# Attention and two feed-forward layers on one core: unsplit gate products in extra places, the second batch's gates ahead of out1, new planner numbers

## The chip, the core and the metric

The kernel runs on one core of a Trainium2 chip. The metric is the device time of one launch in microseconds (us), from several runs; beside it stands one profiled execution, whose trace gives start and duration of every instruction on the five engines: TensorE (PE in the rows, PEld for its weight loads), VectorE (DVE), ScalarE (ACT), GpSimd (POOL) and SyncE (SP, which issues DMA transfers).

## What is computed

```python
a = softmax(phi over the sequence)                    # 4 batches, 8 heads, 576 x 32
k_m, v_m = a^T k, a^T v                               # 32 memory rows of 64 a head
attn = softmax(q k_m^T / 8);  x = attn v_m            # to 2304 tokens x 512
xn = x / rms(x) * rms_g
g, val = xn @ w_gate, xn @ w_val                      # 512 -> 1536
x = (silu(g) * val) @ w_out                           # "out1", 1536 -> 512
h = x @ w_in                                          # 512 -> 2048
out = where(h >= 1, h, where(h <= -1, 0, (h + 1)**2 / 4)) @ w_out2
```

The large weights arrive as 64-bit floats and are converted on the chip.

## The kernel before

Every matmul of full precision is made of three: each operand x is kept as a high part (a copy in the rounded format fp32r) and a low part (x minus that copy), and high*high, high*low and low*high are summed. Splitting an operand is thus a copy on ScalarE and a subtraction on VectorE or GpSimd.

**Stages.** Attention runs first, in nine pairs of column blocks; its end product for batch b is the tiles `Ah{b}`, `Al{b}` (high and low of the attention weights, scaled by the rms; `ATp` are the transposes that lead to them, `xp` the products whose squares give the rms). The values `v_m` are folded into the gate and value weights instead of multiplied with attention: `vw` (L738) makes the folded weights `vwps` of two gate blocks and `vw_parts` splits them into `vwh`, `vwl`. `gv` (L783) then forms, for each of 48 gate blocks n (12 a batch, each of 128 hidden columns) and each half hf of the 576 tokens, six matmuls into `gps` and six into `vps` (L806); `gate` (L814) follows each half: Silu on ScalarE into a tile `th` (L831), times `vps` on VectorE (L834), copy to `ah` on ScalarE (L837), subtraction to `al` (L839). `out1` (L847) sums over the 12 gate blocks of a batch, for four column blocks d4 and two halves, in `ops` (L864: three matmuls a block); `x2_parts` splits the result (L878, L880) and stores it to DRAM. The last phase (L1034, L1065) reads that back for the second feed-forward layer.

**Weights.** `convert` (L236) turns 512 columns of 64-bit floats into 32-bit ones. One transfer fills a `raw` tile (four buffers), then: the high word scaled (L258, VectorE or ScalarE), the low word scaled (L261 or L263, ScalarE or GpSimd), an OR of the two (L267, VectorE), and the sign, either by a second VectorE operation (L272) or by a Sign on ScalarE and a product on GpSimd (L277, L279). Where the weight is needed split, copy (L286) and subtraction (L288, VectorE or GpSimd) follow. The 24 gate and value pieces go to tiles `w` and are also stored to `wf_d`; `load_w` (L728) reloads them for later batches. `wo1` (12 conversions through `cx`) is out1's weight; 32 more conversions through `cx` and the tiles `w2s` are the weights of the last phase, stored to `w2_d` and loaded (L967) on GpSimd's DMA queue.

**Who sets the order.** All of this up to the last phase is written as generators that yield (engine, time) or take and give buffers, banks and flags; `Agenda` plays them against a table of engine times and emits each instruction when its turn comes: earliest start first, then the smaller priority (`P_CONV`, `P_VW`, `P_GV`, `P_OUT1`, `P_W2`). Where a step may run on two engines the earlier end wins, shifted by `BIAS`. So numbers in tables decide the order on every engine, and engines run in that order. A gate takes one of 12 `a` buffers (`ah` and `al` of 576 columns) before its matmuls and a `th` buffer of 288 columns; out1's last column block gives the `a` buffers back one by one. Since 12 gates make a batch, no gate of the next batch starts before out1 has begun its last column block.

## Time and profile before

| what | value |
|---|---|
| median of three runs | 873.9 us (872.69 to 874.95) |
| profiled execution: time, span of its trace | 873.91 us, 872.1 us |
| TensorE busy | 831.8 us, 95% of the span |
| VectorE, ScalarE, GpSimd busy | 472.3 us (54%), 351.1 us (40%), 180.3 us (21%) |
| TensorE clock, mean | 0.975 of full |

The shares are means over stages with different limits: attention and the first batch's gates up to some 185 us, out1 with the later gates up to 470, the second layer from there. Matmuls are pipelined, so a busy TensorE is a TensorE that is never without one, not one at its peak.

### The profile page before, as it was taken

What the parts mean: (1) busy time and instruction counts of PE and PEld (TensorE: products, weight loads), DVE (VectorE), ACT (ScalarE), POOL (GpSimd) and SP (SyncE); (2) the same over time, 40 slices, a digit from 0 to 9 for tenths busy, and PEclk for the clock granted to TensorE, in tenths of its full rate; (3) what the DMA queues carried; (4) which work ended last, traced back from release to release, by engine and by line L of the source; (5) the groups of instructions that cost most, each with busy time, mean ns of one, the idle gap of its engine ahead of it and who ended that gap; (6) DMA issues with size and microseconds to landing.
All of it is one profiled execution on the core that took longest, in us unless ns stands there. A gap on an engine that the chain in (4) does not pass through costs nothing.

```text
span 872.1 us, 15148 instructions
## 1 busy us (share of the span) xinstructions
PE 831.8 (95%) x6058; PEld 725.9 (83%) x6058; DVE 472.3 (54%) x817; ACT 351.1 (40%) x695; POOL 180.3 (21%) x207
## 2 busy tenths in 40 slices
PE   7996797689999999999999999999999999999997
PEld 5885586489999999999999888888888888888896
DVE  3679889984776488448512333433343334333443
ACT  1456686762564367447402222222222222222232
POOL 3257656531231222113302300000000000000000
PEclk9998698799999999999999999999999999999999
DMA  9966666855759668766983960100040002000100
GB/s 318 333 209 188 214 203 229 282 190 200 244 207 318 238 241 271 268 224 242 314 274 121 400 210 1 44 5 1 1 130 16 1 1 72 25 1 1 39 11 24
DMA packets 72199, 137.56 MB, mean 158 GB/s; under 512 B 8897, under 2 KB 37569, under 8 KB 72129
## 3 DMA queue, kind: packets, MB, share of 16 engines
q1 hardware_dynamic: 61472, 108.02, 36.8%
q0 software_dynamic: 10496, 28.32, 10.4%
q8 instruction: 47, 0.77, 0.3%
q10 hardware_dynamic: 160, 0.26, 0.1%
q14 instruction: 24, 0.19, 0.1%
HBM read 99.35 MB, written 37.22 MB: 157 GB/s over the span
## 4 chain that ended last, share of the span: by engine, by line
PE 86%; DVE 6%; ACT 3%; DMA 2%; issue 2%; POOL 1%; SPq 0%; DVEq 0%; ACTq 0%; POOLq 0%
PE acc L1065 23%; PE hp L1034 23%; PE ops L864 17%; PE vps L806 7%; PE gps L806 7%; PE vwps L757 2%; PE xp L678 2%; PE sc L615 1%; DMA kv<-in_v_dram 1%; DMA raw<-in_moe_w_val_dram 1%; PE kvps L489 1%; PE qps L597 1%; DVE w L258 1%; DVE w L267 1%; DVE cx L258 1%
## 5 line engine op out<-in xcount | busy, mean ns | idle before, releaser
L1034 PE MATMUL hp<-xh,w 128*128 128x512 f32 (+1 forms) x640 | 193.1, 368 | 0.0
L1065 PE MATMUL acc<-w,gh 128*128 128x512 f32 x576 | 178.4, 391 | 0.0
L1034 PEld LDWEIGHTS hp<-xh,w 128*128 128x128 f32 x640 | 117.0, 188 | 21.5
L1040 DVE SCALAR_TENSOR_TENSOR y<-y 128x512 f32<-128x512 f32 (+1 forms) x80 | 51.1, 639 | 151.6 <-ACT y L1039 151.6
L1065 PEld LDWEIGHTS acc<-w,gh 128*128 128x128 f32 x576 | 107.0, 188 | 22.4
L1034 PE MATMUL hp<-xl,w 128*128 128x512 f32 (+1 forms) x320 | 118.3, 370 | 0.0
L864 PE MATMUL ops<-ah,wo1h 128*128 128x288 f32 x384 | 113.5, 296 | 0.0
L864 PE MATMUL ops<-ah,wo1l 128*128 128x288 f32 x384 | 113.1, 295 | 0.0
L864 PE MATMUL ops<-al,wo1h 128*128 128x288 f32 x384 | 113.0, 294 | 0.0
L1065 PE MATMUL acc<-w,gl 128*128 128x512 f32 x288 | 112.6, 392 | 0.0
L1039 ACT ACTIVATE y<-hp,consts 128x512 f32<-128x512 f32 (+1 forms) x80 | 51.6, 645 | 151.3 <-PE hp L1034 151.3
L1049 ACT ACTIVATE gh<-y 128x512 fp32r<-128x512 f32 (+1 forms) x80 | 47.4, 593 | 137.7 <-PE acc L1065 120.2
L1050 DVE TENSOR_TENSOR gl<-y,gh 128x512 fp32r<-128x512 f32 (+1 forms) x80 | 51.1, 639 | 80.4 <-ACT gh L1049 80.4
L279 POOL TENSOR_TENSOR cx<-cx,raw 128x512 f32<-128x512 f32 x43 | 58.8, 1368 | 128.3 <-ACT raw L277 92.6
L864 PEld LDWEIGHTS ops<-ah,wo1h 128*128 128x128 f32 x384 | 72.0, 188 | 1.6 <-issue 1.6
L864 PEld LDWEIGHTS ops<-al,wo1h 128*128 128x128 f32 x384 | 72.1, 188 | 0.0
L864 PEld LDWEIGHTS ops<-ah,wo1l 128*128 128x128 f32 x384 | 72.0, 188 | 0.0
L1034 PEld LDWEIGHTS hp<-xl,w 128*128 128x128 f32 x320 | 60.2, 188 | 10.8
L806 PE MATMUL vps<-Ah,vwh 128*128 128x288 f32 x192 | 60.1, 313 | 6.7 <-DVE th L834 6.5
L1065 PEld LDWEIGHTS acc<-w,gl 128*128 128x128 f32 x288 | 54.0, 188 | 12.4
L806 PE MATMUL gps<-Ah,vwh 128*128 128x288 f32 x192 | 59.0, 307 | 5.0 <-ACT vwh L775 3.0
L806 PE MATMUL gps<-Ah,vwl 128*128 128x288 f32 x192 | 58.3, 303 | 3.5 <-DVE vwl L777 3.5
(115 smaller groups left out, 1415.1 us busy)
## 6 DMA issues: line engine op xcount, KB each, us to landing
w<-wf_d SPq DMA_DIRECT2D x36, 512.0 KB, 4.8
w<-w_d POOLq DMA_DIRECT2D x36, 512.0 KB, 9.1
w_d<-w2s SPq DMA_DIRECT2D x32, 512.0 KB, 3.5
raw<-in_moe_w_out_dram SPq DMA_DIRECT2D x28, 512.0 KB, 5.5
raw<-in_moe_w_in_dram SPq DMA_DIRECT2D x16, 512.0 KB, 5.3
raw<-in_moe_w_gate_dram SPq DMA_DIRECT2D x12, 512.0 KB, 4.4
raw<-in_moe_w_val_dram SPq DMA_DIRECT2D x12, 512.0 KB, 4.9
wf_d<-w SPq DMA_DIRECT2D x12, 512.0 KB, 3.0
```

What stands on the lines that cost most here:

```text
L258: nc.vector.tensor_scalar(out=dst, in0=hv, scalar1=SHRINK, scalar2=None, op0=ALU.mult)
L279: nc.gpsimd.tensor_tensor(out=dst, in0=dst, in1=hv, op=ALU.mult)
L678: nc.tensor.matmul(out=xp[rows, 256 * g : 256 * g + 256], lhsT=aT[:, i, g, rows], rhs=vbd_t[bb][:, g].rearrange("p h d -> p (h d)"), start ...
L757: nc.tensor.matmul(out=vps[g][0][32 * c : 32 * c + 32, 2 * P * x : 2 * P * x + 2 * P], lhsT=vT[b][hs, c, :], rhs=t[hs, c].rearrange("p i f ...
L806: nc.tensor.matmul(out=p[:, 0:HB], lhsT=wt[:, g, i, :], rhs=at[b][:, g, c], start=(g == 0 and x == 0), stop=(g == 1 and x == 2),)
L864: nc.tensor.matmul(out=p[:, 0:HB], lhsT=wt[:, fc, d], rhs=at[:, c], start=(fc == 0 and x == 0), stop=(fc == NF1 - 1 and x == 2),)
L1034: nc.tensor.matmul(out=hp, lhsT=wt[:, kc, :], rhs=xt[:, kc, 0:n], start=(kc == 0 and x == 0), stop=(kc == KC - 1 and x == 2),)
L1039: nc.scalar.activation(out=y, in_=hp, func=AF.Relu, scale=0.5, bias=half)
L1040: nc.vector.scalar_tensor_tensor(out=y, in0=y, scalar=1.0, in1=y, op0=ALU.min, op1=ALU.mult)
L1049: nc.scalar.activation(out=gh, in_=y, func=AF.Copy)
L1050: nc.vector.tensor_tensor(out=gl, in0=y, in1=gh.bitcast(F32), op=ALU.subtract)
L1065: nc.tensor.matmul(out=acc, lhsT=gt[:, cs], rhs=wt, start=(fc == 0 and x == 0), stop=(fc == NF2 - 1 and x == 2),)
```

## The change

It has five parts. (1) A gate's product stays unsplit: `gv` takes a `th` place, now of 576 columns, instead of an `a` buffer; the split, now one copy and one subtraction of 576 columns, comes when an `a` buffer is free. Places are two tiles of their own, four halves of batch 0's `Ah0`, `Al0` once its gates are formed (`more_places`), and two `w2s` tiles (`more_w2s`). (2) `wo1`'s conversions wait for gates of the second half of batch 0 or for the first of batch 1 (`WO1_AFTER`), and conversions have a lower priority than folding and gates (`P_CONV` 99 to 850). (3) `BIAS` is set anew; the sign now always goes to VectorE, gate subtractions to GpSimd, softmax scalings and most of `wo1`'s and `w2s`'s subtractions to GpSimd, and 27 of the first 36 high words to ScalarE. `SHARE` makes the planner count some VectorE operations as longer while GpSimd is busy. (4) `W_AFTER` has another starting flag. (5) out1's results are split and stored a half at a time.

```diff
-BUFS = {"phi": 2, "kv": 2, "q": 2, "qr": 1, "pm": 1, "gm": 2, "s1": 2, "kd": 2, "qT": 2, "e": 4, "aT": 3, "half": 1, "raw": 4, "x": 2, "w": 3, "vw": 2, "a": 12, "th": 2, "xs": 2, "w2s": 2}
+BUFS = {"phi": 2, "kv": 2, "q": 2, "qr": 1, "pm": 1, "gm": 2, "s1": 2, "kd": 2, "qT": 2, "e": 4, "aT": 3, "half": 1, "raw": 4, "x": 2, "w": 3, "vw": 2, "a": 12, "th": 2, "xs": 3, "w2s": 2}
...
+SHARE = {"VAhi": 2.1, "VAsign": 1.5, "Vs": 1.5, "VGlo": 1.5, "VGal": 1.5, "GVe": 1.4}
-W_AFTER = [("A", (1, 0)), ("A", (0, 1)), ("e", 1)]
-BIAS = {"VAhi": 98.819, "GAlow": 0, "VGlo": 3.746, "VGsum": -99, "GVe": -2.397, "VGal": 0.2, "VAsign": -0.488, "VGvbd": -0.2}
+W_AFTER = [("e", 2)]
+WO1_AFTER = {(0, 0): ('gv', 6), (1, 0): ('gv', 12), (0, 1): ('gv', 7), (1, 1): ('gv', 12), (0, 2): ('gv', 8), (1, 2): ('gv', 12), (0, 3): ('gv', 9), (1, 3): ('gv', 12), (0, 4): ('gv', 10), (1, 4): ('gv', 12), (0, 5): ('gv', 11), (1, 5): ('gv', 12)}
+BIAS = {"VAhi": -0.0664, "GAlow": -0.3, "VGlo": -0.987, "VGsum": -99, "GVe": 0.8, "VGal": -99, "VAsign": 99, "VGvbd": -0.169}
-P_SOFT, P_PAIR, P_CONV, P_VW, P_GV, P_OUT1, P_W2 = 0, 100, 99, 800, 850, 900, 3000
+P_SOFT, P_PAIR, P_CONV, P_VW, P_GV, P_OUT1, P_W2 = 0, 100, 850, 800, 820, 900, 3000
...
-            yield "take", "a"
+            yield "take", "th"
             hi, lo = vw_t.pop(n)
-            ah = p1.tile([P, S], F32R, tag="ah", name=f"ah{n}", bufs=BUFS["a"])
-            al = p1.tile([P, S], F32R, tag="al", name=f"al{n}", bufs=BUFS["a"])
-            a_t[n] = (ah, al)
+            th_t[n] = th_place(n)
...
+    def th_place(n):
+        if th_free[0] == "w2s":
+            return wv.tile([P, 1024], F32, tag="w2s", name=f"th{n}", bufs=BUFS["w2s"])[:, 0:S], th_free.pop(0)
+        t = th_free.pop(0)
+        return t, t
+    def more_places():
+        yield "flag", ("gv", NF1 - 1)
+        for tag in ("Ah0", "Al0"):
+            t = keep.tile([P, 2, S], F32, tag=tag, name=f"th_{tag}", bufs=1)
+            for z in range(2):
+                th_free.append(t[:, z])
+                yield "give", "th"
...
+        mark(("g", n, hf))
+        if hf == 0:
+            return
+        yield "flag", ("g", n, 0)
+        if n:
+            yield "flag", ("a taken", n - 1)
+        yield "take", "a"
...
-        yield "A", 0.44
+        yield "A", 0.73
         nc.scalar.activation(out=ah, in_=th, func=AF.Copy)
-        eng = yield ("V", 0.46) if n == NT - 1 else ("VGal", (0.46, 0.85))
+        eng = yield ("V", 0.75) if n == NT - 1 else ("VGal", (0.75, 1.6))
...
     def wo1_unit(z, u):
+        if (z, u) in WO1_AFTER:
+            yield "flag", WO1_AFTER[z, u]
```

What the tables make of it is seen in the order of the instructions on the engines. First TensorE where out1 begins (`ops`; `vps` the value half of a gate, `vwps` a folded pair; tiles numbered 93 are batch 0's `Ah`, 94 and 98 batch 1's `Ah` and `Al`). Before:

```order
L806 MATMUL vps_1_2247<-Al_97,vwh_2056 128x288
L806 MATMUL vps_1_2247<-Ah_93,vwl_2057 128x288
L864 MATMUL ops_0_0_2112<-ah_1545,wo1h 128x288
L864 MATMUL ops_0_0_2112<-al_1546,wo1h 128x288
L864 MATMUL ops_0_0_2112<-ah_1545,wo1l 128x288
L757 MATMUL vwps_0_2258<-w_2136,vT_90 32x256 x4
L757 MATMUL vwps_1_2259<-w_2136,vT_90 32x256 x4
L757 MATMUL vwps_0_2258<-w_2167,vT_90 32x256 x4
L757 MATMUL vwps_1_2259<-w_2167,vT_90 32x256 x4
L864 MATMUL ops_0_0_2112<-ah_1616,wo1h 128x288
L864 MATMUL ops_0_0_2112<-al_1617,wo1h 128x288
L864 MATMUL ops_0_0_2112<-ah_1616,wo1l 128x288
```

After:

```order
L814 MATMUL vps_1_2444<-Ah_94,vwh_2229 128x288
L814 MATMUL vps_1_2444<-Al_98,vwh_2229 128x288
L814 MATMUL vps_1_2444<-Ah_94,vwl_2230 128x288
L915 MATMUL ops_0_0_2315<-ah_1488,wo1h 128x288
L915 MATMUL ops_0_0_2315<-al_1489,wo1h 128x288
L915 MATMUL ops_0_0_2315<-ah_1488,wo1l 128x288
L767 MATMUL vwps_0_2453<-w_2317,vT_90 32x256 x4
L767 MATMUL vwps_1_2454<-w_2317,vT_90 32x256 x4
L767 MATMUL vwps_0_2453<-w_2385,vT_90 32x256 x4
L767 MATMUL vwps_1_2454<-w_2385,vT_90 32x256 x4
L915 MATMUL ops_0_0_2315<-ah_1548,wo1h 128x288
L915 MATMUL ops_0_0_2315<-al_1549,wo1h 128x288
```

Before, the last gate ahead of out1's full run is batch 0's twelfth; after, out1's first matmuls stand behind a gate of batch 1. Counted over the whole order, 12 gates and 8 folded pairs stand ahead of out1's 13th matmul before, 18 gates and 11 pairs after. The two places of tag `w2s` serve gates 8 and 9 alone.

Second, VectorE in the stretch in which `wo1` is converted (`cx` a piece on its way, `raw` its 64-bit source, `w` a gate or value piece, `th` a gate product, `al` its low part, `vwl` a folded low part). Before:

```order
L258 TENSOR_SCALAR w_1896<-raw_1959 128x4x128
L839 TENSOR_TENSOR al_1858<-th_1_1940,ah_1857 128x288
L258 TENSOR_SCALAR cx_2019<-raw_1979 128x512
L267 SCALAR_TENSOR_TENSOR w_1896<-w_1896,raw_1959 128x4x128
L839 TENSOR_TENSOR al_1947<-th_0_1982,ah_1946 128x288
L834 TENSOR_TENSOR th_1_2023<-th_1_2023,vps_1_1985 128x288
L267 SCALAR_TENSOR_TENSOR cx_2019<-cx_2019,raw_1979 128x512
L288 TENSOR_TENSOR wo1l<-cx_1958,wo1h 128x2x256
L258 TENSOR_SCALAR cx_2058<-raw_2033 128x512
L839 TENSOR_TENSOR al_1947<-th_1_2023,ah_1946 128x288
L834 TENSOR_TENSOR th_0_2068<-th_0_2068,vps_0_2009 128x288
L267 SCALAR_TENSOR_TENSOR cx_2058<-cx_2058,raw_2033 128x512
```

After:

```order
L870 TENSOR_TENSOR th_Ah_2109<-th_Ah_2109,vps_0_2133 128x288
L787 TENSOR_TENSOR vwl_2114<-vwps_1_2112,vwh_2113 128x512
L277 SCALAR_TENSOR_TENSOR cx_2161<-cx_2161,raw_2097 128x512
L870 TENSOR_TENSOR th_Ah_2109<-th_Ah_2109,vps_1_2173 128x288
L282 SCALAR_TENSOR_TENSOR cx_2161<-raw_2097,cx_2161 128x512
L870 TENSOR_TENSOR th_Ah_2109<-th_Ah_2109,vps_0_2197 128x288
L277 SCALAR_TENSOR_TENSOR cx_2172<-cx_2172,raw_2135 128x512
L282 SCALAR_TENSOR_TENSOR cx_2172<-raw_2135,cx_2172 128x512
L870 TENSOR_TENSOR th_Ah_2109<-th_Ah_2109,vps_1_2218 128x288
L787 TENSOR_TENSOR vwl_2230<-vwps_0_2227,vwh_2229 128x512
L870 TENSOR_TENSOR th_Al_2110<-th_Al_2110,vps_0_2251 128x288
L277 SCALAR_TENSOR_TENSOR cx_2263<-cx_2263,raw_2215 128x512
```

Before, conversions of `w` and `wo1` alternate with gate products and their subtractions of batch 0, and no row has the sign. After, the gate and value pieces are done, each conversion has an OR and a sign (L277, L282), no subtraction of a gate stands here, and the gate products belong to batch 1, in the places of `Ah0` and `Al0`. The first gate product stands at VectorE's row 148 before and at row 131 after.

Third, GpSimd at the same time. Before:

```order
L279 TENSOR_TENSOR w_1709<-w_1709,raw_1814 128x4x128
L279 TENSOR_TENSOR cx_1868<-cx_1868,raw_1828 128x512
L839 TENSOR_TENSOR al_1858<-th_0_1935,ah_1857 128x288
L279 TENSOR_TENSOR w_1896<-w_1896,raw_1912 128x4x128
L279 TENSOR_TENSOR cx_1958<-cx_1958,raw_1933 128x512
L279 TENSOR_TENSOR w_1896<-w_1896,raw_1959 128x4x128
L279 TENSOR_TENSOR cx_2019<-cx_2019,raw_1979 128x512
L279 TENSOR_TENSOR cx_2058<-cx_2058,raw_2033 128x512
```

After:

```order
L888 TENSOR_TENSOR al_1842<-th_1209,ah_1841 128x576
L888 TENSOR_TENSOR al_1895<-th_1210,ah_1894 128x576
L273 TENSOR_SCALAR raw_1897<-raw_1897 128x512
L888 TENSOR_TENSOR al_1942<-th_1866,ah_1941 128x576
L298 TENSOR_TENSOR wo1l<-cx_1935,wo1h 128x2x256
L888 TENSOR_TENSOR al_1994<-th_1910,ah_1993 128x576
L273 TENSOR_SCALAR raw_1938<-raw_1938 128x512
L298 TENSOR_TENSOR wo1l<-cx_1959,wo1h 128x2x256
L888 TENSOR_TENSOR al_2095<-th_1209,ah_2094 128x576
```

Before, GpSimd multiplies signs (L279); after, it subtracts gates of 576 columns (L888) and `wo1`'s low parts (L298).

## Rows read from the trace of the kernel before

**Rows 1.** The windows of five stretches: busy us of each engine (instructions), TensorE clock, DMA.

```profile
61.50:107.60 46.10, 34.70 (x321) 26.65 (x303) 41.91 (x70) 28.69 (x62) 32.99 (x35) 0.74 0.58 183
107.60:134.90 27.30, 24.06 (x229) 20.93 (x214) 24.07 (x44) 23.07 (x50) 16.54 (x15) 1.00 0.62 204
134.90:150.00 15.10, 13.50 (x101) 11.85 (x100) 14.60 (x22) 9.74 (x22) 8.69 (x8) 0.77 0.68 224
150.00:186.00 36.00, 24.60 (x210) 18.80 (x209) 35.70 (x54) 26.01 (x53) 16.59 (x12) 0.86 0.71 239
186.00:470.00 284.00, 284.00 (x2509) 272.82 (x2509) 160.94 (x309) 133.47 (x293) 64.64 (x65) 1.00 0.72 244
```

**Rows 2.** What PE waited for, 105 to 186 us: in total, times, longest.

```profile
PE vps L806 <- DVE th L834: 6.5, 7, 1.6
PE gps L806 <- DVE vwl L777: 3.5, 3, 1.2
PE gps L806 <- ACT vwh L775: 3.0, 1, 3.0
```

**Rows 3.** PE's timeline in the gate stretch: start us, us, line, shape, idle before.

```profile
107.85 0.40 PE L806 MATMUL gps<-Ah,vwh 128*128 128x288 f32 x1
...
110.15 0.66 PE L702 MATMUL ATp<-ident,e 128*128 128x128 f32 x4 [0.45 <-POOL e L694]
...
113.86 1.02 PE L678 MATMUL xp<-vbd,aT 128*128 128x256 f32 x4
...
118.77 1.09 PE L757 MATMUL vwps<-w,vT 64*32 64x256 f32 x32
...
162.55 0.40 PE L864 MATMUL ops<-ah,wo1h 128*128 128x288 f32 x1
...
166.19 0.61 PE L806 MATMUL gps<-Ah,vwh 128*128 128x288 f32 x1 [2.98 <-ACT vwh L775]
```

**Rows 4.** The chain that ended last, two pieces: start us, us, what.

```profile
117.23 0.80 PE gps L806 x6
...
184.73 5.36 PE ops L864 x39
```

**Rows 5.** DVE's groups by form, 61.5 to 186 us: count, busy us, mean ns.

```profile
L267 DVE SCALAR_TENSOR_TENSOR w<-w,raw 128x512 uint32<-128x512 uint32 x24 | 23.1, 962 | 2.8 <-ACT raw L261 2.8
L258 DVE TENSOR_SCALAR w<-raw 128x512 f32<-128x512 f32 x24 | 17.1, 715 | 0.1
L839 DVE TENSOR_TENSOR al<-th,ah 128x288 fp32r<-128x288 f32 x21 | 13.8, 657 | 0.1
L258 DVE TENSOR_SCALAR cx<-raw 128x512 f32<-128x512 f32 x12 | 11.3, 943 | 0.1
...
L288 DVE TENSOR_TENSOR wo1l<-cx,wo1h 128x512 fp32r<-128x512 f32 x10 | 9.0, 903 | 0.0
```

**Rows 6.** Four lines over the whole span: duration ns min, median, max.

```profile
L258 DVE TENSOR_SCALAR w<-raw x24: 411/420/1554, 64.6 to 156.6; 128x512 f32<-128x512 f32 x24
...
L267 DVE SCALAR_TENSOR_TENSOR w<-w,raw x24: 674/693/1792, 66.9 to 158.7; 128x512 uint32<-128x512 uint32 x24
...
L834 DVE TENSOR_TENSOR th<-th,vps x96: 436/447/456, 110.9 to 432.8; 128x288 f32<-128x288 f32 x96
...
L839 DVE TENSOR_TENSOR al<-th,ah x93: 444/452/1544, 114.1 to 433.8; 128x288 fp32r<-128x288 f32 x93
L839 POOL TENSOR_TENSOR al<-th,ah x3: 805/1141/1315, 138.9 to 239.8; 128x288 fp32r<-128x288 f32 x3
```

**Rows 7.** POOL's groups by form, 61.5 to 186 us.

```profile
L279 POOL TENSOR_TENSOR w<-w,raw 128x512 f32<-128x512 f32 x24 | 35.1, 1467 | 25.8 <-ACT raw L277 23.3 <-DVE w L267 1.6 <-DMA raw<-in_moe_w_val_dram 0.8
L279 POOL TENSOR_TENSOR cx<-cx,raw 128x512 f32<-128x512 f32 x11 | 16.4, 1490 | 13.5 <-ACT raw L277 8.9 <-ACT ah L837 2.1 <-ACT vwh L775 1.7
...
L694 POOL TENSOR_TENSOR e<-e,y 128x512 f32<-128x512 f32 x6 | 6.6, 1093 | 0.5
```

**Rows 8.** POOL's timeline where the last phase begins.

```profile
473.51 0.53 POOL L967 DMA_DIRECT2D w<-w_d  x1 [35.92 <-PE hp L1034]
```

More of the change, by code (lines that the diff above doesn't have):

```diff
@@ L78, in _go, with _took @@
         self.live.append(x)
+    def _took(self, kind, engine, t, at):
+        k = SHARE.get(kind, 1.0) if engine == "V" else 1.0
+        other = max(0.0, self.free.get("G", 0.0) - at)
+        return t * k if t * k <= other else t + other - other / k
     def _start(self, x):
@@ L99, in _start @@
         bias = BIAS.get(kind, 0.0)
-        z = min(range(len(times)), key=lambda z: starts[z] + times[z] + (bias if z else 0.0))
+        took = [self._took(kind, e, t, s) for e, t, s in zip(kind, times, starts)]
+        z = min(range(len(times)), key=lambda z: starts[z] + took[z] + (bias if z else 0.0))
         return starts[z], z
@@ L136, in run @@
                 value = kind[z]
-                t = arg[z] if isinstance(arg, tuple) else arg
+                t = self._took(kind, value, arg[z] if isinstance(arg, tuple) else arg, at)
                 if value == "P":
@@ L222, in tile_attn_moe @@
     vT = [keep.tile([P, KC, M], F32, name=f"vT{b}") for b in range(B)]
-    Ah = [keep.tile([P, 2, S], F32R, name=f"Ah{b}") for b in range(B)]
-    Al = [keep.tile([P, 2, S], F32R, name=f"Al{b}") for b in range(B)]
+    Ah = [keep.tile([P, 2, S], F32R, tag=f"Ah{b}", name=f"Ah{b}", bufs=1) for b in range(B)]
+    Al = [keep.tile([P, 2, S], F32R, tag=f"Al{b}", name=f"Al{b}", bufs=1) for b in range(B)]
     agenda = Agenda({**BUFS, **{("bank", z): 1 for z in range(8)}})
@@ L265, in convert @@
             )
-        yield "V", 0.69
+        yield "Vs", 0.69
         nc.vector.scalar_tensor_tensor(
@@ L809, in gv, with more_w2s, gate @@
                             )
-                add(P_GV, gate(n, hf, ps, ah[:, c], al[:, c]))
+                add(P_GV, gate(n, hf, ps))
+            mark(("gv", n))
             if n % 2:
                 yield "give", "vw"
-    def gate(n, hf, ps, ah, al):
-        yield "take", "th"
+    th_t = {}
+    th_free = []
+    def th_place(n):
[10 more added lines that the diff above has]
+                yield "give", "th"
+    def more_w2s():
+        yield "flag", ("w begun", NF1 - 1)
+        for _ in range(BUFS["w2s"]):
+            yield "take", "w2s"
+            th_free.append("w2s")
+            yield "give", "th"
+    def gate(n, hf, ps):
+        c = slice(HB * hf, HB * hf + HB)
         yield "A", 0.41
-        th = p1.tile([P, HB], F32, tag="th", name=f"th{n}_{hf}", bufs=BUFS["th"])
+        th = th_t[n][0][:, c]
         if nexp[0]:
@@ L835, in gate @@
         yield "give", ps[1][1]
-        yield "A", 0.44
+        mark(("g", n, hf))
[5 more added lines that the diff above has]
+        yield "take", "a"
+        mark(("a taken", n))
+        ah = p1.tile([P, S], F32R, tag="ah", name=f"ah{n}", bufs=BUFS["a"])
+        al = p1.tile([P, S], F32R, tag="al", name=f"al{n}", bufs=BUFS["a"])
+        a_t[n] = (ah, al)
+        th, place = th_t.pop(n)
+        yield "A", 0.73
         nc.scalar.activation(out=ah, in_=th, func=AF.Copy)
-        eng = yield ("V", 0.46) if n == NT - 1 else ("VGal", (0.46, 0.85))
+        eng = yield ("V", 0.75) if n == NT - 1 else ("VGal", (0.75, 1.6))
         (nc.vector if eng == "V" else nc.gpsimd).tensor_tensor(
@@ L841, in gate @@
         )
-        yield "give", "th"
-        mark(("a", n, hf))
-        if n == NT - 1 and hf:
+        if isinstance(place, str):
+            yield "give", "w2s"
+        else:
+            th_free.append(place)
+            yield "give", "th"
+        for z in range(2):
+            mark(("a", n, z))
+        if n == NT - 1:
             mark("gates")
@@ L850, in out1 @@
                 yield "flag", ("wo1", d4 // 2)
-                yield "take", "xs"
-                xh = p1x.tile([P, S], F32R, tag="xh", name=f"xh{b}_{d4}", bufs=BUFS["xs"])
-                xl = p1x.tile([P, S], F32R, tag="xl", name=f"xl{b}_{d4}", bufs=BUFS["xs"])
                 for hf in range(2):
@@ L902, in wo1_unit @@
         src = src.rearrange("(c p) f -> p c f", p=P)
-        return convert(src, 2, None, (wo1h[:, fs, c], wo1l[:, fs, c]), done)
+        yield from convert(src, 2, None, (wo1h[:, fs, c], wo1l[:, fs, c]), done)
     wo1_left = [NF1 // 2, NF1 // 2]
@@ L947, in tile_attn_moe @@
     p1 = pool(left, "p1", "left")
+    th_free += [p1.tile([P, S], F32, name=f"th_{z}") for z in range(BUFS["th"])]
     add(P_GV, gv())
+    add(P_SOFT, more_places())
+    add(P_W2 - 1, more_w2s())
     agenda.run("attention")
```

32 lines of the change are left out of this document (17 added, 15 removed).

## Prediction

> **What bounds the kernel now.** I read the windows by stage first. From 186 to 470 us TensorE is busy 284.00 of 284.00 us at the full clock [rows 1]: out1, the later gates and all that lies beside them are TensorE's, and the last phase behind them is a chain of matmuls as well. Nothing on another engine can shorten that part. What can be shortened lies ahead of 186: there TensorE is busy 34.7 of 46.1, 24.1 of 27.3, 13.5 of 15.1 and 24.6 of 36.0 us, and in three of these four stretches its clock is below full speed, 0.74, 0.77 and 0.86, that is, part of the time at 1.2 instead of 2.4 GHz [rows 1]. The second reading is TensorE's waits from 105 to 186: the gate product on VectorE (6.5 us), the low half of the folded weights on VectorE (3.5 us), the high half on ScalarE (3.0 us) [rows 2]. The third is VectorE itself: 41.9 + 24.1 + 14.6 + 35.7 = 116.3 us busy of the 124.5 us from 61.5 to 186 [rows 1]. So VectorE bounds the stretch in which TensorE starves. Last come the places in TensorE's timeline: first gate at 107.85, a first triple of out1 at 162.55 with ten gates done, then a wait of 2.98 us [rows 3], and out1 without a gap from 184.73 [rows 4], with twelve gates done and twelve matmuls of out1.
>
> **The change on TensorE.** The order puts the gates of n = 12 to 17, batch 1's, ahead of out1. The words of the change say 8 places, but the two of tag w2s serve n = 8 and 9 only and go to other weights then; six unsplit gates is what lies ahead. Six matmuls of a gate take 0.80 us from their first to the next six [rows 4], so a gate (24) takes 3.2 us and six gates 19.0 (at 0.79). Three folded weight pairs come along, 1.09 us each [rows 3]: 3.3 us. So 22.2 us of TensorE work move from behind 184.7 to ahead of it, while what follows is full before and after. If T is the time at which out1 has twelve matmuls and runs on without a gap (184.7 before), the end moves by (184.7 + 22.2) - T = 206.9 - T. Everything hangs on T.
>
> **T from VectorE.** Counted over the order, from the start to out1's first eviction, VectorE's work of the kinds that change is, before and after, with undisturbed durations (the medians of [rows 6]; 0.69 us for each two-input operation of 512 columns, as L267): high halves of converted weights 36 and 9 at 0.42 (15.1, 3.8 us); the OR with the low bits 36 and 36 (24.8, 24.8); the sign 0 and 35 (0, 24.2); gate products 24 and 36 at 0.447 (10.7, 16.1); gate low halves 22 and 0 at 0.452 (9.9, 0); folded low halves 16 and 22 (11.0, 15.2); wo1's low halves 12 and 1 (8.3, 0.7); the softmax scaling 9 and 1 (6.2, 0.7). The sums are 86.0 and 85.5 us. VectorE is not relieved; it does the work of 18 gates instead of 12 in the same undisturbed time, because the sign came over and the low halves went away.
>
> The durations are disturbed, though. In this stretch the rows exceed their medians: L267 on w 962 against 693 ns, x24, 6.5 us; L258 on w 715 against 420, x24, 7.1 us; L839 657 against 452, x21, 4.3 us; L258 on cx 943 against 420, x12, 6.3 us; L288 903 against 690, x10, 2.1 us [rows 5, 6]. That is 26.3 us of blocking. The product L834, which reads PSUM, never takes more than 456 ns [rows 6], so what blocks is on the SBUF side, and the engine that is busy there beside VectorE is POOL, with 33.0 + 16.5 + 8.7 + 16.6 = 74.8 us in the stretch [rows 1], of which the 35 sign products are 35.1 + 16.4 = 51.5 us [rows 7]. These leave. What comes is 12 gate low halves of 576 columns (twice a 288-column one, whose three rows are 805, 1141 and 1315 ns [rows 6]: 1.6 to 2.6 us; I take 1.7, since the 512-column products of [rows 7] are at 1.48 and 9/8 of that is 1.67), so 20.4 us; five of wo1's low halves at 1.48, 7.4 us; five softmax scalings at 1.1 as L694 [rows 7], 5.5 us. POOL goes to 56.6 us, 0.76 of before, and blocking in proportion to 19.9 us: 6.4 us less. Ends: nothing less, and 9 us less (two-input operations alone, 60 to 40 us). VectorE is through at about 186 - 0.5 - 6.4 = 179 us, 176 to 186.
>
> The rule of the Trainium skill's page GPSIMD Engine Reference, section 3.1, that elementwise work belongs on VectorE because GpSimd takes about twice as long, speaks against moving the gate low halves. This trace agrees on the ratio for one row alone (452 against 805 to 1315 ns [rows 6]). By it those subtractions would stay where they were, and T would be later by the 9.9 us that they took on VectorE; the sum above is worked out without it.
>
> **T from TensorE.** From the first gate to T it has to do 18 gates (56.9 us at 3.16), nine folded pairs (9.8 us), attention's last three transposes (0.66 each) and two products (1.02 each) [rows 3] (4.0 us), twelve matmuls of out1 (1.6 us): 72.3 us. With the first gate at 107.85 and no gap that is 180.1. Two corrections: the first gate product now stands at VectorE's row 131 instead of 148, 5.9 us less of undisturbed work ahead of it, which I count half (start at 105, ends 102 and 107.85); and gates on TensorE ran at 24.06 of 27.30 us, 88%, in the one stretch at the full clock [rows 1]. VectorE's 179 and TensorE's 177 (105 + 72.3) lie so near each other that neither will be met: at 92%, between 88 and 100, T = 105 + 72.3/0.92 = 184. Ends: 174 (102, no gap) and 198 (107.85, 80%).
>
> **The rest of the change** I cost at nothing, and name the cover. wo1's conversions wait for gates 6 to 12; in VectorE's order the first six are done two gates and more ahead of out1 and the last one stands just behind its first eviction, and out1 reads that half after 144 matmuls, 19 us; if it is not ready, TensorE waits. The deferred splits: as out1's last column block frees a buffer, ScalarE splits and POOL subtracts, at 1.7 us each against 3.2 us of TensorE per new gate; without that cover a place is late by at most an operation of POOL, some 2 us at each of three batch ends. The two halves of x2 go out in smaller stores, each under 36 matmuls (4.7 us). The last phase's weights load later, behind POOL's subtractions, but POOL's queue had nothing to issue for 35.9 us ahead of that phase [rows 8]. So the sum is 206.9 - 184 = 22.9 us. The profiled execution took 873.91 us with a span of 872.1, the median is 873.9; 873.9 - 22.9 = **851.0 us**.
>
> **Rivals.**
> First, *VectorE stays disturbed.* POOL's subtractions at 2.6 us (the upper end) put POOL at 67 us, 0.90 of before, and the sign on VectorE is one more operation with two SBUF inputs that can be blocked. T comes to 190 to 203: 857 to 870 us. For it: the medians hide operations of up to 1.8 us [rows 6]. Against it: 51.5 us of POOL leave.
> Second, *the pace of before holds.* The ten gates ahead of 162.55 took 54.7 us, 5.5 us each with their weights [rows 3]. If conversions (four raw buffers, as before) and not VectorE set that pace, 18 gates need 99 us: T = 107.85 + 99 + 1.6 = 208, 875 us, no change.
> Third, on the other side, *the two-place ring.* Up to n = 7 a gate's first step on ScalarE overwrites a place that POOL must have read two gates earlier, and POOL stands behind VectorE: matmuls 3.2, two blocked operations of VectorE ahead of the product 3.6 (2 x 1.79), product 0.45, subtraction 2.6, an allowance of 1.3 for the copy on ScalarE and the hand-overs: 11.1 us for two places, 5.6 us a gate, and behind the waiting ScalarE instruction stand the weights' copies of the next gates, so that the lateness goes on. The point from which it decides is (206.9 - 1.6 - 107.85)/18 = 5.4 us a gate. Before, all twelve took 6.4 us each (76.9/12). At 5.9, T = 216: 883 us. The Trainium skill's page SBUF — State Buffer, section Who interferes with whom, says that whichever of a two-input VectorE operation and a GpSimd operation starts first blocks the other fully; that is how POOL's 805 could become 1315 ns. Against it: only 8 of 18 gates use the ring of two.
>
> **How the numbers follow.** Forecast, T 178 to 190 (845 to 857 us): 0.62. T under 178: 0.08. First rival (857 to 870): 0.16. Second, or a gain given back later: 0.05. Third (over 876.5): 0.09. A measurement of this kernel tells 0.3%, 2.6 us, from no change. Faster 0.86, same 0.05, slower 0.09. The range of 843 to 867 holds the forecast, half of the case under 845 and three quarters of the first rival, 0.78.
>
> **What would show it.** The gap-free out1 begins near 184 us with 18 gates done; TensorE's waits from 105 to T are under 8 us; VectorE's L277 and L282 rows have means near 0.85 us; 284 us full from T on less the 22 moved. Wrong: out1 past 195, or waits of TensorE on ScalarE's gate behind POOL, or new waits at the batch ends.

## The result, and the profile after

The changed kernel takes 853.53 us (median of four runs, 851.52 to 855.04) against 874.41 us of the kernel before in the same series: ratio 0.977, 95% interval 0.976 to 0.979. The forecast was 851.0. The profiled execution took 853.51 us with a span of 851.7, so the spans differ by 20.4 us.

The windows of the kernel after, over the five stretches of [rows 1]; columns: stretch and its length, busy us of PE, PEld, DVE, ACT and POOL with instructions, granted clock, DMA share, GB/s:

```profile
61.50:107.60 46.10, 38.56 (x421) 30.55 (x403) 40.91 (x73) 35.96 (x78) 26.04 (x32) 0.93 0.62 195
107.60:134.90 27.30, 25.19 (x256) 22.39 (x255) 25.79 (x39) 17.41 (x37) 12.80 (x10) 1.00 0.75 239
134.90:150.00 15.10, 12.03 (x127) 9.44 (x126) 13.92 (x19) 10.20 (x20) 7.42 (x6) 0.99 0.96 343
150.00:186.00 36.00, 36.00 (x354) 33.11 (x353) 32.18 (x48) 23.63 (x50) 19.88 (x16) 0.96 0.84 288
186.00:470.00 284.00, 280.34 (x2341) 266.70 (x2341) 146.08 (x227) 117.84 (x235) 116.44 (x100) 1.00 0.74 247
```

Against [rows 1] TensorE idles less ahead of 186 us (12.7 us instead of 27.6), though not in every stretch: from 134.9 to 150 us it idles 3.1 us, where it was 1.6. The granted clock there is 0.93 to 1.00, where it was 0.74 to 1.00. After it, where it was full before, 3.7 us are now missing, and GpSimd has 116 us of work instead of 65. TensorE's timeline after (start us, us, shape, idle before it in brackets, none here), at the first gate and at out1's beginning:

```profile
95.76 0.40 PE L814 MATMUL gps<-Ah,vwh 128*128 128x288 f32 x1
...
180.34 1.09 PE L767 MATMUL vwps<-w,vT 64*32 64x256 f32 x32
181.36 0.40 PE L915 MATMUL ops<-ah,wo1h 128*128 128x288 f32 x1
...
182.52 0.29 PE L915 MATMUL ops<-ah,wo1l 128*128 128x288 f32 x1
182.65 0.29 PE L915 MATMUL ops<-ah,wo1h 128*128 128x288 f32 x1
```

The first gate starts at 95.8 us (107.85 in [rows 3]), and the twelfth matmul of out1 starts at 182.52 us with 18 gates done: T, the start of the thirteenth, is 182.65 us. In the kernel before, the thirteenth starts at 185.16 us; at the 184.7 of the prediction nine were done there, not twelve:

```profile
185.16 0.30 PE L864 MATMUL ops<-ah,wo1h 128*128 128x288 f32 x1
```

What TensorE waited for from 95 to 183 us (total, times, longest):

```profile
PE vps L814 <- DVE th L870: 2.5, 3, 1.4
PE vwps L767 <- DVE vwl L787: 2.3, 2, 1.4
PE aTp L667 <- POOL raw L273: 1.6, 1, 1.6
...
```

And from 186 to 470 us:

```profile
PE vps L814 <- DVE th_Al L870: 3.4, 4, 1.4
PE vps L814 <- DVE th L870: 0.3, 1, 0.3
```

These are new: 3.7 us at three batch ends (1.7, 0.9 and 1.1), where TensorE had no idle time before. VectorE's timeline ahead of the first of these waits (TensorE stands 1.4 us until 231.23):

```profile
223.99 1.91 DVE L277 SCALAR_TENSOR_TENSOR cx<-cx,raw 128x512 uint32<-128x512 uint32 x1
...
226.55 1.21 DVE L282 SCALAR_TENSOR_TENSOR cx<-raw,cx 128x512 uint32<-128x512 uint32 x1
227.68 1.93 DVE L298 TENSOR_TENSOR w2s<-cx,w2s 128x512 fp32r<-128x512 f32 x1
...
230.74 0.44 DVE L870 TENSOR_TENSOR th_Al<-th_Al,vps 128x288 f32<-128x288 f32 x1
```

GpSimd's timeline at the same time (in brackets its idle time before, and what ended it):

```profile
221.61 3.74 POOL L888 TENSOR_TENSOR al<-th,ah 128x576 fp32r<-128x576 f32 x2
225.31 1.90 POOL L888 TENSOR_TENSOR al<-th_Ah,ah 128x576 fp32r<-128x576 f32 x1
227.43 1.64 POOL L888 TENSOR_TENSOR al<-th_Ah,ah 128x576 fp32r<-128x576 f32 x1 [0.21 <-ACT ah L886]
```

GpSimd's deferred subtractions stand back to back; beside them the conversions on VectorE take 1.2 to 1.9 us instead of 0.7, and the product that TensorE waits for stands behind them. VectorE's groups by form, 61.5 to 182.6 us (count, busy us, mean ns):

```profile
L282 DVE SCALAR_TENSOR_TENSOR w<-raw,w 128x512 uint32<-128x512 uint32 x24 | 24.3, 1017 | 0.3
L277 DVE SCALAR_TENSOR_TENSOR w<-w,raw 128x512 uint32<-128x512 uint32 x24 | 20.8, 874 | 0.1
L282 DVE SCALAR_TENSOR_TENSOR cx<-raw,cx 128x512 uint32<-128x512 uint32 x10 | 12.0, 1196 | 0.1
```

GpSimd's subtractions in the same stretch:

```profile
L888 POOL TENSOR_TENSOR al<-th,ah 128x576 fp32r<-128x576 f32 x12 | 19.4, 1618 | 21.2 <-ACT ah L886 21.1
```

**Where the 20.4 us came from.** A span is TensorE's busy time plus its idle time. Every run's trace has 6058 matmul records, so both can be compared between kernels. Idle time here is a window's length less PE's busy time; "elsewhere" is what is left of span less busy time.

| kernel | median us | ratio to before, 95% | idle 61.5–182.6 | idle 182.6–470 | elsewhere | TensorE busy |
|---|---|---|---|---|---|---|
| before | 874.4 | | 27.7 | 0.0 | 12.7 | 831.8 |
| after | 853.5 | 0.976–0.979 | 12.7 | 3.7 | 12.6 | 822.7 |
| two places only | 861.0 | 0.985–0.988 | 15.1 | 8.4 | 12.8 | 822.7 |
| places, all old tables | 873.0 | 0.998–1.000 | 25.6 | 1.7 | 12.8 | 832.1 |
| old biases | 880.8 | 1.005–1.011 | 18.9 | 11.5 | 19.1 | 831.2 |
| every sign on GpSimd | 894.7 | 1.023–1.026 | 21.8 | 10.4 | 32.0 | 829.5 |
| gate lows on VectorE | 851.3 | 0.974–0.978 | 18.8 | 1.4 | 13.0 | 816.4 |
| lows at batch ends on VectorE | 856.2 | 0.977–0.982 | 13.0 | 7.5 | 14.1 | 821.8 |
| no sign, planned anew | 853.9 | 0.975–0.981 | 13.3 | 2.9 | 13.5 | 821.1 |
| conversions first | 862.7 | 0.986–0.989 | 20.5 | 1.7 | 12.4 | 824.1 |
| sign on 64 columns, same order | 843.1 | 0.963–0.969 | 8.9 | 0.4 | 12.5 | 818.3 |
| sign twice, same order | 886.4 | 1.012–1.017 | 26.6 | 14.0 | 13.4 | 831.5 |
| out1's second half later | 854.1 | 0.974–0.980 | 12.4 | 3.8 | 12.7 | 825.1 |
| gate lows on VectorE, high words on ScalarE | 853.6 | 0.977–0.981 | 12.4 | 4.2 | 12.9 | 821.1 |

The change saves 14.9 us of idle time ahead of out1 and gives 3.7 back. The other 9.1 us are busy time: the same matmuls ran shorter. The granted clock of 61.5 to 182.6 us rose from 0.83 to 0.96, that is, less of the stretch was at 1.2 GHz; how much of the 9.1 us that explains was not measured apart. Part of it can also be fewer stops: matmuls that start 0.13 us apart are listed with 0.29 us each, so each stop adds the rest of its last matmul to the busy time.

### The profile page after: what moved, and what is told of

Its sections match the earlier page's. It is cut to its first block, busy times and chain, and to the rows that moved or that the text cites. A ratio compares the mean times of both kernels' runs of the same rounds, so it can differ in the third digit from the quotient of the medians.

```text
span 851.7 us, 14955 instructions
## 1 busy us (share of the span) xinstructions
PE 822.7 (97%) x6058; PEld 720.0 (85%) x6058; DVE 444.5 (52%) x711; ACT 328.2 (39%) x622; POOL 217.2 (26%) x223
## 3 DMA queue, kind: packets, MB, share of 16 engines
q0 software_dynamic: 10496, 28.32, 10.4%
## 4 chain that ended last, share of the span: by engine, by line
PE 86%; DVE 6%; issue 3%; ACT 2%; DMA 2%; POOL 1%; SPq 0%; DVEq 0%; POOLq 0%; ACTq 0%
PE acc L1124 23%; PE hp L1093 23%; PE ops L915 18%; PE vps L814 7%; PE gps L814 6%; PE vwps L767 2%; PE sc L625 2%; PE xp L688 1%; PE heat L479 1%; DMA raw<-in_moe_w_in_dram 1%; PE kvps L499 1%; DMA raw<-in_moe_w_out_dram 1%; DVE cx L277 1%; DVE w L282 1%; DVE cx L282 1%
## 5 line engine op out<-in xcount | busy, mean ns | idle before, releaser
L1124 PEld LDWEIGHTS acc<-w,gl 128*128 128x128 f32 x288 | 54.0, 188 | 12.4
L1065 POOL DMA_DIRECT2D xl<-x2l_d x5 | 3.7, 746 | 221.3 <-PE hp L1093 219.8
L814 PE MATMUL gps<-Al,vwh 128*128 128x288 f32 x192 | 57.2, 298 | 0.0
```

What stands on the lines that cost most here:

```text
L814: nc.tensor.matmul(out=p[:, 0:HB], lhsT=wt[:, g, i, :], rhs=at[b][:, g, c], start=(g == 0 and x == 0), stop=(g == 1 and x == 2),)
L1124: nc.tensor.matmul(out=acc, lhsT=gt[:, cs], rhs=wt, start=(fc == 0 and x == 0), stop=(fc == NF2 - 1 and x == 2),)
```

## The experiments

**Which part brings the gain: places or tables?** The first run takes the six extra places away and keeps the new tables; the second keeps the places and sets the planner's tables back.

```diff
-    add(P_SOFT, more_places())
-    add(P_W2 - 1, more_w2s())
```

> The six extra places are taken away, the two own ones stay; all new numbers stay. Before out1's thirteenth matmul stand 14 gates and 9 folded pairs instead of 18 and 11: 4 gates (12.7 us of TensorE) and 2 pairs (2.2 us) go behind out1's start. Theory (VectorE bounds the stretch, out1 waits for its weights): VectorE loses 8 products and 4 folded low halves, 6.4 us undisturbed, some 8 us as disturbed as in the changed kernel; out1 runs on from about 175 us and the time is 853.5 - 7.6 + 14.9 = 861 us. Rival (TensorE's pace of 83% holds whatever it does): out1 from about 165 us, 850.5 us, that is, the places bring nothing. Rival (the places bring all they move): out1 from 182.6 as before, 868 us.

Measured: 861.0 us, at the theory's number but not by its path. Out1 has its thirteenth matmul at 164.1 us, where the first rival had it (165) and not the theory (175):

```profile
164.14 0.30 PE L915 MATMUL ops<-ah,wo1h 128*128 128x288 f32 x1
```

The time is lost behind that; TensorE's waits in that run from 182.6 to 470 us:

```profile
PE gps L814 <- ACT th L867: 2.6, 3, 2.1
PE vps L814 <- DVE th L870: 2.4, 3, 1.6
PE ops L915 <- DVE xl L933: 1.6, 1, 1.6
PE ops L915 <- POOL wo1l L298: 1.3, 2, 0.9
PE ops L915 <- ACT wo1h L296: 0.4, 1, 0.4
```

Out1's weights account for 1.7 of these 8.4 us; most of the rest are waits of the gates that are left for later. That the number agrees with the theory's is chance.

```diff
-SHARE = {"VAhi": 2.1, "VAsign": 1.5, "Vs": 1.5, "VGlo": 1.5, "VGal": 1.5, "GVe": 1.4}
+SHARE = {}
...
-W_AFTER = [("e", 2)]
-WO1_AFTER = {(0, 0): ('gv', 6), ...}
-BIAS = {"VAhi": -0.0664, ..., "GVe": 0.8, "VGal": -99, "VAsign": 99, ...}
+W_AFTER = [("A", (1, 0)), ("A", (0, 1)), ("e", 1)]
+WO1_AFTER = {}
+BIAS = {"VAhi": 98.819, ..., "GVe": -2.397, "VGal": 0.2, "VAsign": -0.488, ...}
...
-P_SOFT, P_PAIR, P_CONV, P_VW, P_GV, P_OUT1, P_W2 = 0, 100, 850, 800, 820, 900, 3000
+P_SOFT, P_PAIR, P_CONV, P_VW, P_GV, P_OUT1, P_W2 = 0, 100, 99, 800, 850, 900, 3000
```

> The unsplit gates with all places and the stores in halves stay; the tables (biases, shares, priorities, starting flags, flags of out1's weights) are those of the kernel before. Theory: VectorE has the 86 us of the kernel before, and 12 products and 6 folded low halves more (9.5 us), as disturbed as before (26 us), so out1 with 18 gates done runs on at about 184.7 + 12 = 197 us: 868 us. Rival (the places alone make the gain, the tables nothing): 852 to 856 us. Rival (without the tables nothing is gained): 872 to 876 us.

Measured: 873.0 us. The places alone gain nothing that can be told from no change; here the theory's 868 was too low and the rival "without the tables nothing" held. The first gate is back at 108.2 us and the idle time ahead of out1 at 25.6 us. The order differs, too: 10 gates stand ahead of out1's thirteenth matmul, the other eight come between matmuls of out1, and with 18 gates done out1 runs on only from 208 us. So the tables (with the two own places) are worth 12.7 us (873.7 to 861.0), the places alone 0.8, and the places on top of the tables 7.5 (861.0 to 853.5).

**Who should do the sign and the subtractions?**

```diff
-BIAS = {..., "VAsign": 99, ...}
+BIAS = {..., "VAsign": -99, ...}
```

> In the changed kernel every sign goes back to a Sign on ScalarE and a product on GpSimd. VectorE loses 35 operations of 0.69 us (24 us) ahead of out1, GpSimd gets 35 of 1.47 us (51 us). Theory (GpSimd's work blocks VectorE and is itself late): GpSimd would be busy some 116 of the 121 us, the gate subtractions and out1's weights stand behind signs, VectorE's gain is eaten: 856 to 866 us. Rival (VectorE's own count decides): out1 from about 172 us, 843 us.

Measured: 894.7 us, 41 us slower than the change; the direction is the theory's, the size is not. Neither expectation had the place where the largest part goes. TensorE's waits from 440 us on:

```profile
PE hp L1093 <- DMA xh<-x2h_d: 26.7, 1, 26.7
```

And the chain that ended last there (start us, us, what):

```profile
462.20 8.92 DMA w_d<-w2s
...
472.15 4.78 DMA w<-w_d
...
477.21 12.83 DMA xl<-x2l_d
```

With signs on GpSimd the conversions for the last phase end so late that their last stores leave at 462 us; the loads of `w_d` wait for them on GpSimd's queue, and the loads of out1's result stand behind those. TensorE stands still from 463 us on. The window ahead of the table's 470 us (columns as above) has 9.2 us of idle time already:

```profile
450.00:470.00 20.00, 10.79 (x82) 10.56 (x80) 2.44 (x5) 3.10 (x6) 5.32 (x7) 0.87 0.69 220
```

So the wait lies on both sides of 470 us. Of the 42.0 us between the spans, some 26 are this wait (19.4 in the table's "elsewhere", 32.0 less 12.6, and 6.7 ahead of 470 us), 9.1 are idle time ahead of out1, and 6.8 longer busy time. So the main cost is the late queue; what GpSimd's blocking costs this run does not show apart.

```diff
-BIAS = {..., "VGal": -99, ...}
+BIAS = {..., "VGal": 99, ...}
```

> In the changed kernel the gate subtractions go to VectorE (0.75 us each, 12 of them ahead of out1: 9 us more; GpSimd loses 19.4 us there). Theory (blocking goes with GpSimd's busy time): 6.9 us of VectorE's blocking leave, net 2 us later; the TensorE waits of 3.7 us at the three batch ends, which come from VectorE being blocked by these very subtractions, go away: 851 to 853 us. Rival (VectorE's count decides): 9 us later, 860 to 862 us.

Measured: 851.3 us, by the theory, though its interval overlaps the change's. VectorE's groups by form in this run, 61.5 to 182.6 us:

```profile
L282 DVE SCALAR_TENSOR_TENSOR w<-raw,w 128x512 uint32<-128x512 uint32 x24 | 18.4, 770 | 0.2
L282 DVE SCALAR_TENSOR_TENSOR cx<-raw,cx 128x512 uint32<-128x512 uint32 x10 | 9.3, 931 | 0.1
L888 DVE TENSOR_TENSOR al<-th,ah 128x576 fp32r<-128x576 f32 x12 | 9.1, 754 | 1.6 <-ACT ah L886 1.6
```

VectorE took 9.1 us of subtractions on and was still less busy (104.8 us against 111.1): with 13.3 us less of GpSimd beside them its signs fell from 1017 to 770 and from 1196 to 931 ns, and the planner gave it three high words fewer (2.1 us of them instead of 6.0). Waits at the batch ends fell from 3.7 to 1.4 us. A good part was lost again at one place, in the chain that ended last:

```profile
133.89 8.52 issue
...
142.45 2.27 POOL wo1l L298
...
144.74 0.43 DVE cx L268
...
146.13 0.68 DVE vwl L787
```

VectorE's high word of the next piece waits for one of the two `cx` buffers, and the folded low half that TensorE needs stands behind it. TensorE's longest wait there is 5.0 us; in 135 to 150 us it idles 7.8 us in all.

```diff
-        eng = yield ("V", 0.75) if n == NT - 1 else ("VGal", (0.75, 1.6))
+        eng = yield ("V", 0.75) if n == NT - 1 or n >= NF1 and n % NF1 < 6 else ("VGal", (0.75, 1.6))
```

> In the changed kernel the gate subtractions of the six gates that are formed ahead of the next batch's out1 (18 of 48) go to VectorE, the others stay on GpSimd. Theory (GpSimd's back-to-back subtractions at a batch's end block VectorE's conversions, behind which a gate product stands): TensorE's 3.7 us of waits at the batch ends go, 849.8 to 851 us. Rival (18 operations of 0.75 us more on VectorE are late themselves): 853 to 856 us.

Measured: 856.2 us, at the rival's upper end; the theory's gain did not come. The idle time after 182.6 us is 7.5 us instead of 3.7, and its largest part is now a wait on ScalarE (182.6 to 470 us):

```profile
PE gps L814 <- ACT th_Al L867: 3.5, 3, 2.0
```

Moving a part of the subtractions was no better than moving none or all. Why ScalarE's gates come late in this order was not followed further.

```diff
-BIAS = {"VAhi": -0.0664, "GAlow": -0.3, "VGlo": -0.987, "VGsum": -99, "GVe": 0.8, "VGal": -99, "VAsign": 99, "VGvbd": -0.169}
+BIAS = {"VAhi": 98.819, "GAlow": 0, "VGlo": 3.746, "VGsum": -99, "GVe": -2.397, "VGal": 0.2, "VAsign": -0.488, "VGvbd": -0.2}
```

> The changed kernel with the old biases alone: signs mostly on GpSimd, gate and folded lows on VectorE where the earlier end is, all high words on VectorE, softmax scaling on VectorE; places, flags, shares and priorities stay as changed. Theory (who does the split and the sign is what counts; the run with every sign on GpSimd took 894.7 us, the one with all old tables 873.0): 868 to 876 us. Rival (order and flags count, since 18 gates still stand ahead of out1's seventh matmul): 853 to 860 us.

Measured: 880.8 us, slower than the kernel before. The direction is the theory's, past its range: as with all signs on GpSimd there is a wait ahead of the last phase (16.2 us for out1's result), and the first gate is at 103.0 us. So the new order and flags do not carry the gain without the new shares of work between engines.

**Is VectorE the bound?** First without the sign at all:

```diff
-        eng = yield "VAsign", (0.69, 0.68)
...
+        eng = "none"
```

> The changed kernel without any sign of the converted weights: the operation is left out (the output is therefore another), 35 operations of VectorE go ahead of out1. Theory (VectorE bounds what lies ahead of out1): 24 us of undisturbed work and 13 us of its blocking leave; what remains is TensorE's own work, which idles 12.7 us of the 121.1 us from 61.5 to 182.6 in the changed kernel and loses some 5 us at the low clock; so out1 runs on 10 to 17 us earlier, 836 to 844 us. Rival (the transfers of the raw weights set the pace): 850 to 854 us.

Measured: 853.9 us, the rival's number: with VectorE busy 84.3 us instead of 111.1 in 61.5 to 182.6 us nothing was gained. By itself this would have ended the theory. But the planner had put everything in another order: the first gate at 81.8 us, and 7.4 us idle in 61.5 to 95.8 us where the change has 4.8. What bounds that order was not followed. Two more runs therefore keep the planner's numbers and the order, instruction for instruction, and change only what VectorE does when the sign's turn comes.

```diff
+            hu = hv.bitcast(U32)
+            ds, hs = (t[:, :, 0:16] if len(dst.shape) > 2 else t[:, 0:64] for t in (du, hu))
             nc.vector.scalar_tensor_tensor(
-                out=du, in0=hv.bitcast(U32), scalar=0x80000000, in1=du,
+                out=ds, in0=hs, scalar=0x80000000, in1=ds,
```

> The changed kernel, instruction for instruction in the same order, but VectorE's sign works on 64 of the 512 columns (the other columns lose their sign, so the output is another). The kernel without signs took 853.9 us, but its planner made another order; this one keeps the order. Theory (VectorE's work bounds the stretch ahead of out1): some 20 us of undisturbed work leave it there, TensorE's idle time (12.7 us in 61.5 to 182.6) and low clock shrink, 838 to 845 us. Rival (other steps, transfers and the order of waits, set the pace; VectorE's load has slack): 850 to 854 us.

```diff
-            nc.vector.scalar_tensor_tensor(
+            for _ in range(2):
+              nc.vector.scalar_tensor_tensor(
```

> The changed kernel in the same order, but VectorE does every sign twice (the second changes nothing): 35 more operations of 0.69 us or more ahead of out1, 33 more behind. Theory (VectorE bounds): 24 to 36 us later, 878 to 890 us. Rival (slack): up to 10 us later, 855 to 863 us.

Measured: 843.1 and 886.4 us, both at the theory. With 35.4 us less of VectorE's time in the whole span (409.1 against 444.5) the time falls by 10.4 us; with 53.7 more (498.2) it rises by 32.8. TensorE's largest waits from 30 to 190 us with the short sign:

```profile
PE vwps L769 <- DVE vwl L789: 2.2, 2, 1.3
PE sc L627 <- ACT kmT L568: 1.8, 2, 1.3
PE aTp L669 <- ACT th L869: 1.6, 1, 1.6
```

And from 182.6 to 470 us with the double one:

```profile
PE vps L815 <- DVE th_Ah L871: 7.3, 5, 3.3
PE vps L815 <- DVE th_Al L871: 4.4, 4, 1.7
```

With the short sign no wait on a gate product is left among them, the chain runs into out1 without a gap from 173.7 us (181.4 after), and the batch ends cost 0.4 us; doubled, the products are late there too. By the same mark T is 174.9 us with the short sign, 182.65 in the change and 203.3 with the double one. So in this order VectorE's work sets T and has no slack. It is not the only bound: a microsecond of it is worth less downwards (0.29) than upwards (0.61). That fits the forecast's second bound, TensorE's own work, but was not shown apart; with the short sign TensorE still idles 8.9 us ahead of 182.6 us, on other waits.

**The earlier first gate, and the transfers.**

```diff
-P_SOFT, P_PAIR, P_CONV, P_VW, P_GV, P_OUT1, P_W2 = 0, 100, 850, 800, 820, 900, 3000
+P_SOFT, P_PAIR, P_CONV, P_VW, P_GV, P_OUT1, P_W2 = 0, 100, 99, 800, 820, 900, 3000
```

> The changed kernel with the old priority of conversions (ahead of the attention pairs and of folding and gates) alone. In VectorE's order the first gate product stands at row 147 instead of 131. Theory (the total of VectorE's work ahead of out1 sets T, not when the first gate comes): first gate at 102 to 108 us instead of 95.8, time within 4 us of 853.5. Rival (the earlier first gate is where the gain comes from): 860 to 866 us.

Measured: 862.7 us, the rival's number: with conversions ahead of attention's pairs the first gate comes at 101.4 us and the change loses 9.2 us. Its window of attention's end:

```profile
61.50:95.80 34.30, 24.39 (x238) 16.53 (x237) 30.67 (x60) 24.18 (x51) 13.27 (x16) 0.80 0.80 261
```

The same window of the change:

```profile
61.50:95.80 34.30, 29.52 (x374) 22.67 (x355) 31.02 (x55) 26.31 (x57) 21.07 (x27) 0.95 0.60 188
```

VectorE is as busy in both; what it does differs. TensorE loses 5.1 us there and its clock falls to 0.80. Over 61.5 to 182.6 us VectorE is even less busy than in the change (96.6 us against 111.1), and T comes at 190.9. So VectorE's total ahead of T is not all: late attention cost more here than the early conversions gave back. The planner has made another order here as well, so the loss belongs to the order as a whole.

```diff
-WO1_AFTER = {..., (1, 0): ('gv', 12), ..., (1, 1): ('gv', 12), ..., (1, 2): ('gv', 12), ..., (1, 3): ('gv', 12), ..., (1, 4): ('gv', 12), ..., (1, 5): ('gv', 12)}
+WO1_AFTER = {..., (1, 0): ('gv', 15), ..., (1, 1): ('gv', 15), ..., (1, 2): ('gv', 16), ..., (1, 3): ('gv', 16), ..., (1, 4): ('gv', 17), ..., (1, 5): ('gv', 17)}
```

> In the changed kernel the six conversions of the second half of out1's weights wait for gates 15, 16 and 17 instead of 12. Theory (from 135 to 150 us the DMA engines are 0.96 busy and TensorE idles 3.1 us, because these conversions' transfers and the weights of batch 1's gates come together): TensorE's idle time there falls under 1 us, and VectorE's 12 us for them go behind out1's start: 848 to 851 us. Rival (they are late for out1's third column block or push the conversions for the last phase back): a new wait of TensorE after 185 us, 855 to 860 us.

Measured: 854.1 us (849.95 to 855.65), neither theory: no new wait on out1's weights, and the idle time from 135 to 150 us stays at 2.9 us. It stood at 3.1 after, 2.7 with the short sign. The chain of this run shows the same piece as the change's (there 7.03 us from 135.93), a transfer of out1's weights of the first half:

```profile
136.95 7.04 DMA raw<-in_moe_w_out_dram
```

The second half was not what filled the DMA engines there (0.98 busy in this run). Whether a fifth `raw` buffer would start that transfer earlier was not tried.

**A version from these runs.**

```diff
-BIAS = {"VAhi": -0.0664, ..., "VGal": -99, ...}
+BIAS = {"VAhi": -99, ..., "VGal": 99, ...}
```

> A version from what the runs showed: the gate subtractions on VectorE as in the run of that edit (851.3 us, without waits of more than 1.4 us at the batch ends), and every high word of a converted weight on ScalarE. Against that run VectorE loses all its high words (25 of the lines' 36 and 32 conversions, 0.43 us each, 4 of them gate and value pieces) and with them the place where it waited from 143.6 to 144.7 us for a buffer of out1's weights. Theory (VectorE's work ahead of out1 sets the time, 0.4 to 0.5 us of time for each us of it): 845 to 850 us. Rival (ScalarE, which then waits for that buffer with gates behind it, takes VectorE's part): new waits of TensorE on ScalarE, 853 to 860 us.

Measured: 853.6 us, no better than the change. The edit did what it was for (idle 12.4 instead of 18.8 us ahead of 182.6, 2.3 instead of 7.8 in 135 to 150), but TensorE's busy time rose from 816.4 to 821.1 us, and the last phase now waits for out1's result. The waits from 186 to 470 us:

```profile
PE hp L1093 <- DMA xl<-x2l_d: 2.3, 1, 2.3
...
```

The expectation's 0.4 to 0.5 us for each microsecond of VectorE's work, which lies between the 0.29 and 0.61 of the two runs of fixed order, does not carry over to an edit after which the planner orders everything anew.

## Why the prediction was right, and where it was not

**The form of the sum held.** 206.9 less T of 182.65 is 24.2 us; 3.7 given back at the batch ends leave 20.5, and the spans differ by 20.4. Agreement to 0.1 us is chance: with 185.16 as the kernel before's mark the sum gives 21.0, so it holds to about half a microsecond. The forecast of 22.9 was high by 2.5: T came 1.35 us earlier than taken, and the rest that was costed at nothing took 3.7.

**T from TensorE was near by luck: two errors cancel.** The start was put at 105 us, ends 102 and 107.85, and was 95.8. The step that failed is the half of VectorE's 5.9 us: it counted rows ahead of the first product and did not see that the new priority puts attention's own work ahead of conversions. Taking back that priority alone moves the first gate by 5.6 us (95.8 to 101.4), taking back the biases alone by 7.2 (to 103.0); the prediction gave both together 2.85. The share of 92%, ends 88 and 100, was 72.3/86.85, or 83%. Of the 14.5 us beyond 72.3, TensorE's waits are 7.9 (95.8 to 182.6 us, 86.8 long, has 78.86 busy), just under the 8 that the prediction allowed; the other 6.6 are matmuls longer than the work had been counted at, part of them at the low clock, as the clock of 0.93 up to 107.6 us and 0.96 from 150 on shows. The share had been read from the one stretch at full clock [rows 1].

**T from VectorE was right in direction and nearly in size.** It was to fall from 116.3 us by 6.9 (0.5 and 6.4) to 109.4; from 61.5 to T it is 111.1. That VectorE's work moves T in this order is shown by the two runs of fixed order. GpSimd did not fall to 56.6 us but to 64.5: the gate subtractions came at 1.62 us where 1.7 was taken, but the weights' low parts on it were nine (13.1 us) and not five (7.4), the low words that it scales were 13 instead of the nine before (10.6 us, 7.2 before), and the softmax scalings took 1.3 instead of 1.1. Blocking, by the means of L282 and L277 over an undisturbed 693 ns, is 20.5 us for these alone (7.8 and 4.3 for `w`, 5.0 and 3.4 for `cx`), where 19.9 was forecast for all; the high words left on VectorE (L268) add 2.6. The means of L277 and L282 were to be near 0.85 us and are 0.87 to 1.20. (The 26.3 us of before left out the OR on `cx`, another 1.6.)

**The rule of the GPSIMD page.** By the Trainium skill's GPSIMD Engine Reference, section 3.1, the gate subtractions would have stayed on VectorE. The ratio agrees again (1618 against 754 ns), and the run that keeps them there takes 851.3 us, not measurably less than the change. The 9.9 us that the prediction put on it did not appear: T is 183.5 us there. With 13.3 us less of GpSimd VectorE's signs and ORs were shorter by another 9.9 us (24 by 247 ns, 24 by 37, 10 by 265, 11 by 39), as much as the 9.1 us that came; the order changed as well, so the cause is likely and not shown apart. The run that breaks the rule for the sign took 41 us more, some 26 of them by the late loads of the last phase.

**What was costed at nothing.** The cover at the batch ends was thin, and the bound given ("some 2 us at each") was of the right size: 1.7, 0.9 and 1.1. The mechanism was another: no place was late, but VectorE's conversions for the last phase, blocked by the deferred subtractions, stood ahead of the product. With the subtractions off GpSimd 1.4 us of idle time are left there, with VectorE's sign shortened in the same order 0.4; part of the subtractions moved gave 7.5, so the number of GpSimd's operations alone does not settle it. The cover of the last phase's weights held, with no wait there in the change; that GpSimd's queue can be late is shown by the runs with signs on GpSimd (26.7 and 16.2 us).

**The rivals.** VectorE disturbed to T of 190 and more: T was 182.65, though the premise nearly came: GpSimd was busy 64.5 us (the rival had 67) and blocking was 23.1 us and more, nearer to 0.90 of 26.3 than to the forecast's 19.9. The subtractions took 1.62 us, not 2.6. What neither had is the first gate at 95.8 us. The pace of before, 5.5 us a gate: it was (182.65 - 95.8)/18 = 4.8. The two-place ring: no wait of TensorE on a gate's first step behind GpSimd is in the list, and 4.7 us a gate (4.8 less out1's 1.6 us over 18) is below its point of 5.4. The second rival's kernel exists, though: with the old tables the places alone give 873.0 us. The prediction priced the change as a whole and could not have said that the tables with two places give 12.7 us of it and the places without the tables nothing.

## What to carry to other kernels

Where numbers in a table let a planner order every engine, test a cost with the planner's number left in place and the instruction itself shortened or doubled: leaving the operation out made another order, whose 853.9 us said nothing about this one. Room to run ahead (places, buffers) gains only what the engine that feeds it can use; here the places were worth 0.8 us with the old tables and 7.5 with the new. Split a span into TensorE's busy and idle time by stage: 9.1 of the 20.4 us here were shorter busy time of the same matmuls, which no wait shows.
